# A Trainium2 attention and MoE kernel: the second MoE layer by seven half products, with scaled inputs and one buffer of streaming rows

One core of one Trainium2 chip. The metric is the device time of one launch in microseconds (us); a kernel's time is the median of its runs. PE is TensorE (PEld its weight loads), DVE VectorE, ACT ScalarE, POOL GpSimd; SP is the engine that only issues DMAs here. Groups of tokens and their attentions are numbered from 0: "the second attention" is that of group 2, "the third" that of group 3, and "the second chunk" is group 1. "Turned" means transposed.

## The reference, cut to what matters

```python
# attention: B=4, H=8, S=768, D=64; heads 0, 2, 6 see all earlier rows ("retrieval"),
# the other five see 4 sink rows and a window of 64 rows ("streaming")
x = attention(q, k, v).transpose(0, 2, 1, 3).reshape(3072, 512)
# MoE: E=4 experts, w1[e] 512 x 1024, w2[e] 1024 x 512
p = probs / (probs.sum(-1, keepdims=True) + 1e-9)
for e in range(4):
    h = np.maximum(x @ w1[e], 0.0)
    out += p[:, e:e+1] * (h @ w2[e])
```

## The kernel before

The tokens go in eight groups of 384 (half of a batch entry), three tiles of 128 each. While PE computes the MoE of group g, single steps of the attention of group g+1 are put between its matmuls, paced by a plan. The MoE part:

```python
for g, e in units:                              # 8 groups x 4 experts
    for ft in range(8):                         # first layer: 4 matmuls of 384 columns each
        ... matmul(out=ps[:, 0:384], lhsT=w1sb[...], rhs=xT[g][:, ct, :]) x4
        nc.scalar.activation(out=hs[:, ft, :], in_=ps[:, 0:CH], func=AF.Relu)
    for j in range(3):                          # second layer, tile by tile
        ... matmul(out=ps_o, lhsT=hs[:, ft, tile j], rhs=w2sb[:, e*FTP+ft, :]) x8   # 512 columns
        acc[nt] = p[nt, e] * ps_o (+ acc[nt])   # DVE, one for each tile and expert
```

The attention's data come by cast-loads (they change the type on the way) from POOL's queue and are turned by DMA transposes from SP's queue. The parts (cut):

```python
def dma_transposes(b, c):                # SP: sinks of kSr, q -> qT, kRr -> kR, kSr -> kS
def loads(g2):                           # POOL: k, q, v of group g2
for g in range(G):
    att_steps = attention(g + 1)
    loads(g + 2)
    begin = {0: 1.15, 1: 1.0}.get(g, 0.0) * UNIT     # UNIT: one group and expert, 10.4 us of PE
    end = {0: 3.5}.get(g, 0.90 * n_units) * UNIT
    for ns, share in moe_steps(units[g]):
        ...                              # run attention steps while done < planned share
```

Streaming keys and values have two buffers, q two.

The softmax here doesn't subtract the row's maximum and nothing guards it: scores larger than these inputs give would overflow.

Of the kernel before, what the change touches and what calls it, by code (L numbers as in the profile page):

```python
# [17 lines left out]
def kernel(  # L18
# [34 lines left out]
    P = 128  # L53
# [50 lines left out]
    NR, NSH = len(RH), len(SH)  # L104
    kR = []
    kSf = []
    vR = []
    vSf = []
    for i in range(2):
        kR.append(pers.tile([P, NCH, NR, 3, P], FP16, name=f"kR{i}"))  # L110
        kSf.append(pers.tile([P, NCH * TC * NSH * P], FP16, name=f"kS{i}"))
        vR.append(pers.tile([P, S // P, NR, D + 2], FP16, name=f"vR{i}"))
        vSf.append(pers.tile([P, NT * NSH * P], FP16, name=f"vS{i}"))

    kS = kSf[0].rearrange("p (c s t x) -> p c t s x", c=NCH, t=TC, s=NSH)
    vS = vSf[0].rearrange("p (c s t x) -> p c t s x", c=NCH, t=TC, s=NSH)

    def windows(x, c):

        return x[1 - c][:, 0 : WT * NSH * P].rearrange(  # L120
            "p (t s x) -> p t s x", t=WT, s=NSH
        )

    ident32 = pers.tile([P, P], FP32, name="ident32")
    ident16 = pers.tile([P, P], FP16, name="ident16")
    warm = pers.tile([P, 512], FP16, name="warm")
    bC = pers.tile([P, 2 * P], FP16, name="bC")
    bS = pers.tile([P, 3, TQ], FP16, name="bS")
# [4 lines left out]
    mW = pers.tile([P, WT + 2, WQ], FP16, name="mW")  # L133
# [8 lines left out]
    k_sinks = pers.tile([NS, 1, NSH * P], FP16, name="k_sinks")  # L142
    v_sinks = pers.tile([NS, 1, NSH * P], FP16, name="v_sinks")
# [16 lines left out]
    def key_tile(b, c, h, t):  # L160

        i = b % 2
        if RETR[h]:
            return kR[i][:, t // 3, RH.index(h), t % 3, :]
        if b:
            return windows(kSf, c)[:, t, SH.index(h), :]
        return kS[:, t // TC, t % TC, SH.index(h), :]

    def v_tiles(b, c, h):

        if RETR[h]:
            return vR[b % 2][:, 3 * c : 3 * c + 3, RH.index(h), :]
        if b:
            return windows(vSf, c)[:, :, SH.index(h), :]
        return vS[:, c, :, SH.index(h), :]
# [30 lines left out]
    def load_q(b, c):  # L206
        q16[b, c] = att.tile([P, 3, H, D], FP16, name="q16", bufs=2)
        load_by_rows(q, q16[b, c], b, c)
# [10 lines left out]
    def load_k(b, c):  # L219

        for h in range(H):
# [26 lines left out]
    def dma_transposes(b, c):  # L248
        i = b % 2
        put_sinks(kSr, k_sinks, c)  # L250
        alloc_qT(b, c)
# [6 lines left out]
        for x, xr in ((kR[i][:, c, :, :, :], kRr), (windows(kSf, c), kSr)):  # L258
            nc.sync.dma_start(
                out=x.rearrange("p t s x -> p (t s) x"),  # L260
                in_=xr.rearrange("p t s x -> p (t s x)"),
                transpose=True,
            )
# [24 lines left out]
    def sink_rows(b, c):  # L288
        if b:
            put_sinks(windows(vSf, c), v_sinks, c)  # L290
            return
# [43 lines left out]
    def one_values(eng, c):  # L335

        one_values_r(eng, 0, c)
        x = vS[:, c, :, :, :].rearrange("p t s x -> p s t x")
        fill(eng, x[0:R0, :, :, :].rearrange("p s t x -> p (s t x)"), ONES)
        fill(eng, x[:, 0:2, :, D:P], ONES)  # L340
        fill(eng, x[:, 2:5, :, 0:D], ONES)
# [5 lines left out]
    q32 = moe.tile([P, 3, H, D], FP32, name="q32", tag="hs", bufs=2)  # L347
    k32 = moe.tile([P, 3, H, D], FP32, name="k32", tag="hs", bufs=2)

    v_s32 = pers.tile([NS, H, D], FP32, name="v_s32")  # L350
# [29 lines left out]
    zero(nc.vector, kS[:, 0, :, :, :].rearrange("p t s x -> p s t x"))  # L380
# [42 lines left out]
    def mask_w():  # L423

        gp.memset(mW, 1.0)
# [27 lines left out]
    zero(gp, kS[:, 1, :, :, :].rearrange("p t s x -> p s t x"))  # L453
    one_values(gp, 1)
    k16 = att.tile([P, H, 3, D], FP16, name="k16", bufs=1)
    qt16 = att.tile([P, H, 3, D], FP16, name="q16", bufs=2)
# [38 lines left out]
    def attention(b, c):  # L495
# [3 lines left out]
        xT[g] = att.tile([P, HP, CH], FP16, name="xT", bufs=2)  # L499
# [105 lines left out]
        def scores(h):  # L605
            hp = h // 2
            es_of[h] = []
            for cols, parts, masks in score_tiles(h):
# [22 lines left out]
                es = att.tile([P, 512], FP16, name="es", bufs=12)  # L631
# [77 lines left out]
        def values(h):  # L709
# [31 lines left out]
            if not pair or u == 0:  # L741
                rc_of[0] = att.tile([P, CH], FP32, name="rc", bufs=4)
# [61 lines left out]
        else:  # L804
            sink_rows(b, c)
            order = (0, 2, 6, 1, 3, 5, 7, 4) if by_dma else (0, 2, 1, 3, 6, 5, 7, 4)
            if not by_dma:
# [4 lines left out]
            for n, h in enumerate(order):  # L812
                v_steps = iter(())
                if len(waiting) > (0 if by_dma else 1):
                    v_steps = values(waiting.pop(0))
                yield from both(scores(h), v_steps)
                waiting.append(h)
                if not by_dma and n in (1, 3):
                    yield from transposes({1: 3, 3: 2}[n])
            for h in waiting:  # L820
                yield from values(h)

# [21 lines left out]

    behind = []
# [11 lines left out]
    def last_tile(e, nt, hs, acc):  # L857

        for n, eng in enumerate((nc.sync, nc.scalar)):
            cols = slice(n * DM // 2, (n + 1) * DM // 2)  # L860
            ps = pV.tile([P, 512], FP32, name="pV", bufs=2)
            for ft in range(FTP):
                nc.tensor.matmul(
                    out=ps[:, 0 : DM // 2],
                    lhsT=hs[:, ft, 2 * P : 3 * P],
                    rhs=w2sb[:, e * FTP + ft, cols],
# [3 lines left out]
            nc.vector.scalar_tensor_tensor(  # L870
                out=acc[:, cols], in0=ps[:, 0 : DM // 2],
                scalar=p_sb[:, nt, e : e + 1], in1=acc[:, cols],
                op0=ALU.mult, op1=ALU.add,
            )
            eng.dma_start(out=out[nt * P : (nt + 1) * P, cols], in_=acc[:, cols])


    acc = {}

    def moe_steps(units):  # L880
        for g, e in units:
            nt0 = g * 3
            hs = moe.tile([P, FTP, CH], FP16, name="hs", tag="hs", bufs=2)


            ahead = 4 if g == 0 and e == 0 else 1
            for f0 in [0, *range(ahead, FTP)]:
                pss = {ft: bank() for ft in range(f0, f0 + (1 if f0 else ahead))}


                cts = (0, 2, 1, 3) if g == 0 else (2, 1, 3, 0)

                def layer1(ft, n):
                    ct = cts[n]
                    nc.tensor.matmul(  # L895
                        out=pss[ft][:, 0:CH],
                        lhsT=w1sb[:, e * DMP + ct, ft * P : (ft + 1) * P],
                        rhs=xT[g][:, ct, :],
                        start=(n == 0),
                        stop=(n == DMP - 1),  # L900
                    )

                for ft in pss:
                    for ct in range(DMP - 1):
                        layer1(ft, ct)
                for ft, ps in pss.items():
                    layer1(ft, DMP - 1)
                    nc.scalar.activation(  # L908
                        out=hs[:, ft, :], in_=ps[:, 0:CH], func=AF.Relu
                    )  # L910
                    yield DMP * mm_ns(CH), 0.6
            for j in range(3):
                nt = nt0 + j
                if g == G - 1 and e == E - 1 and j == 2:
                    last_tile(e, nt, hs, acc[nt])
                    continue
                ps_o = pO.tile([P, DM], FP32, name="pO", bufs=2)
                for ft in range(FTP):
                    nc.tensor.matmul(  # L919
                        out=ps_o,  # L920
                        lhsT=hs[:, ft, j * P : (j + 1) * P],
                        rhs=w2sb[:, e * FTP + ft, :],
                        start=(ft == 0),
                        stop=(ft == FTP - 1),
                    )
                    if ft == FTP // 2 - 1:
                        yield FTP // 2 * mm_ns(DM), 1.4
                p_ap = p_sb[:, nt, e : e + 1]
                if e == 0:
                    acc[nt] = moe.tile([P, DM], FP32, name="acc", bufs=6)  # L930
                    nc.vector.tensor_scalar(  # L931
                        out=acc[nt], in0=ps_o, scalar1=p_ap, scalar2=None, op0=ALU.mult
                    )
                else:
                    nc.vector.scalar_tensor_tensor(  # L935
                        out=acc[nt], in0=ps_o, scalar=p_ap, in1=acc[nt],
                        op0=ALU.mult, op1=ALU.add,
                    )
                if e == E - 1:
                    nc.sync.dma_start(out=out[nt * P : (nt + 1) * P, :], in_=acc[nt])  # L940
                yield FTP // 2 * mm_ns(DM), 1.4
# [10 lines left out]
    mask_w()  # L952

    units = {g: [(g, e) for e in range(E)] for g in range(G)}

    def loads(g2):
# [79 lines left out]
```

## Time and profile before

| | before |
|---|---|
| median time | 399.19 us (398.47 to 400.19, 3 runs) |
| span of the profiled run | 397.1 us, clock 1.000 |
| PE, PEld, DVE, ACT, POOL busy | 98%, 56%, 39%, 55%, 36% |

The busy shares, the stretches and the bare pace of the matmuls are shown and read in the prediction below. One more number is used throughout, and is worked out from the trace: for each matmul the time to the start of the next one, less columns/2.4 + 2.5 ns. I call the sum of columns/2.4 + 2.5 **issue**, and the rest **lost**. Before: 385.1 us of issue, 12.0 us lost, 4.9 of it in the first 22 us and 3.6 after the last matmul. One thing in these figures is not as that rule says: the 24 fp32 transposes of the first 22 us were counted with four times their columns, though they go by in some 109 ns each (median), twice what 128 columns take. Counted plainly, 3.8 us move from issue to lost (before: 381.3 and 15.7 us).

### The profile page before, as it was taken

The numbers are of one execution on the slowest core, as the hardware profiler recorded it, in microseconds if no ns is written. First come the engines' busy times: TensorE is split into PE (matmuls) and PEld (weight loads), VectorE is DVE, ScalarE is ACT, GpSimd is POOL, SyncE is SP. The second block draws the span as 40 slices with busy tenths as digits, with TensorE's granted clock in tenths as the row PEclk, the third lists the DMA queues.
The fourth block names the chain that finished last, engine by engine and source line by source line (L and its number), as shares of the span: only waits on it lengthen the run. The fifth ranks groups of instructions, "written<-read, shape, count | busy, mean of one in ns | idle before, by whom it ended". The sixth has DMA issues, their size and how long they took to land.

```text
span 397.1 us, 7140 instructions
## 1 busy us (share of the span) xinstructions
PE 388.2 (98%) x2829; PEld 220.7 (56%) x2829; DVE 156.0 (39%) x344; ACT 219.0 (55%) x468; POOL 143.7 (36%) x184
## 2 busy tenths in 40 slices
PE   7899999999999999999999999999999999999996
PEld 4654556545555555555555555555555555555553
DVE  7734765324442234434332333433443223422222
ACT  4754569444766546655765446745564456853331
POOL 8833796808908706900049202940000000000000
PEclk9999999999999999999999999999999999999999
DMA  9999999999999999970779959990472000020002
GB/s 172 158 208 192 178 197 172 139 199 128 128 191 149 121 149 106 141 90 12 141 80 175 65 99 118 112 153 12 83 117 83 2 12 1 11 79 2 0 2 80
DMA packets 166133, 42.23 MB, mean 106 GB/s; under 512 B 156396, under 2 KB 161108, under 8 KB 166100
## 3 DMA queue, kind: packets, MB, share of 16 engines
q0 software_dynamic: 102656, 20.98, 62.0%
q1 hardware_dynamic: 61700, 20.27, 26.5%
q10 hardware_dynamic: 1744, 0.52, 0.6%
q8 instruction: 22, 0.36, 0.4%
q14 instruction: 11, 0.09, 0.1%
HBM read 43.57 MB, written 6.29 MB: 126 GB/s over the span
## 4 chain that ended last, share of the span: by engine, by line
PE 78%; DMA 15%; POOL 6%; issue 1%; DVE 0%; POOLq 0%
PE pA L895 35%; PE pO L919 35%; DMA w1sb<-in_moe_w_dram 4%; DMA w2sb<-in_moe_w_dram 4%; PE pA L614 4%; DMA q<-in_q_dram 3%; DMA kR<-kRr 2%; POOL vR L269 2%; PE pV L726 1%; PE pV L662 1%; DMA vS<-in_v_dram 1%; POOL w1sb L300 1%; POOL vS L275 1%; POOL vS L326 0%; POOL q L201 0%
## 5 line engine op out<-in xcount | busy, mean ns | idle before, releaser
L895 PE MATMUL pA<-xT,w1sb 128*128 128x384 f16 x1024 | 185.9, 326 | 0.1
L919 PE MATMUL pO<-w2sb,hs 128*128 128x512 f16 x760 | 179.0, 379 | 0.8 <-DMA w2sb<-in_moe_w_dram 0.8
L908 ACT ACTIVATE hs<-pA 128x384 f16<-128x384 f32 x256 | 121.8, 492 | 94.9 <-PE pA L895 89.6
L895 PEld LDWEIGHTS <-w1sb 128*128 128x128 f16 x1024 | 95.8, 98 | 59.6 <-issue 0.5
L919 PEld LDWEIGHTS <-hs 128*128 128x128 f16 x760 | 70.7, 98 | 73.9 <-DMA w2sb<-in_moe_w_dram 1.2
L632 ACT ACTIVATE es<-pA 128x384 f16<-128x384 f32 (+2 forms) x122 | 60.1, 512 | 53.7 <-PE pA L614 52.4
L935 DVE SCALAR_TENSOR_TENSOR acc<-pO,p_sb,acc 128x512 f32<-128x512 f32 x71 | 53.3, 751 | 71.8 <-PE pO L919 71.3
L227 POOL DMA_DIRECT2D kSr<-in_k_dram x30 | 30.1, 1006 | 31.5 <-DMA kS<-kSr 22.1
L223 POOL DMA_DIRECT2D kRr<-in_k_dram x18 | 14.1, 785 | 67.7 <-DMA kR<-kRr 67.7
L749 DVE TENSOR_TENSOR xT<-pV,rc 64x384 f16<-64x384 f32 x37 | 20.5, 554 | 32.0 <-ACT rc L754 24.3
L271 POOL DMA_DIRECT2D vS<-in_v_dram x30 | 30.4, 1024 | 0.8 <-DMA q<-in_q_dram 0.8
L931 DVE TENSOR_SCALAR acc<-pO,p_sb 128x512 f32<-128x512 f32 x24 | 18.0, 751 | 28.8 <-PE pO L919 28.6
L636 DVE TENSOR_TENSOR es<-es,mC 128x256 f16<-128x256 f16 (+1 forms) x42 | 10.9, 258 | 45.4 <-ACT es L632 44.3
L744 ACT ACTIVATE rc<-pV,eps 64x384 f32<-64x384 f32 x37 | 21.3, 575 | 12.1 <-PE pV L726 11.5
L614 PE MATMUL pA<-qT,kR 128*128 128x384 f16 (+2 forms) x120 | 24.4, 278 | 0.9 <-ACT qT L525 0.4
L754 ACT ACTIVATE rc<-rc 64x384 f32<-64x384 f32 x38 | 19.8, 521 | 1.2
L269 POOL DMA_DIRECT2D vR<-in_v_dram x24 | 19.2, 802 | 0.4 <-issue 0.3
L726 PEld LDWEIGHTS <-vS 128*128 128x128 f16 x255 | 13.4, 98 | 7.7 <-DMA vS<-in_v_dram 2.1
L636 DVE TENSOR_TENSOR es<-es,mW 128x384 f16<-128x384 f16 x30 | 10.7, 358 | 16.9 <-ACT es L632 16.8
L614 PEld LDWEIGHTS <-kR 128*128 128x128 f16 x120 | 11.4, 98 | 10.6 <-DMA kR<-kRr 0.6
L662 PEld LDWEIGHTS <-es 128*128 128x128 f16 x252 | 13.2, 97 | 6.9 <-ACT es L632 0.6
L614 PEld LDWEIGHTS <-kS 128*128 128x128 f16 x255 | 13.3, 98 | 6.6
(102 smaller groups left out, 188.4 us busy)
## 6 DMA issues: line engine op xcount, KB each, us to landing
out_dram<-acc SPq DMA_DIRECT2D x23, 256.0 KB
w1sb<-in_moe_w_dram POOLq DMA_DIRECT2D x8, 512.0 KB, 9.4
w2sb<-in_moe_w_dram POOLq DMA_DIRECT2D x4, 1024.0 KB, 13.2
kSr<-in_k_dram POOLq DMA_DIRECT2D x30, 112.0 KB, 3.8
vS<-in_v_dram POOLq DMA_DIRECT2D x30, 112.0 KB, 5.6
q<-in_q_dram POOLq DMA_DIRECT2D x18, 128.0 KB, 4.3
vR<-in_v_dram POOLq DMA_DIRECT2D x24, 48.0 KB, 4.4
kRr<-in_k_dram POOLq DMA_DIRECT2D x18, 48.0 KB, 3.7
```

The costliest lines, as they stand in the source:

```text
L227: gp.dma_start(out=kSr[:, :, SH.index(h), own(h)], in_=windows_of(k, b, h, c),)
L269: gp.dma_start(out=t[:, :, 0:D], in_=rows_of(v, b, h, c))
L271: gp.dma_start(out=t[:, :, own_v(h)], in_=windows_of(v, b, h, c))
L614: nc.tensor.matmul(out=ps[:, o : o + nq], lhsT=key_tile(b, c, h, t), rhs=qTs[b, c][:, hp, q0 : q0 + nq], start=(n == 0 or not first), stop ...
L632: nc.scalar.activation(out=es[:, 0:cols], in_=ps[:, 0:cols], func=AF.Exp, scale=SC)
L636: nc.vector.tensor_tensor(out=es[:, o0:o1], in0=es[:, o0:o1], in1=m[:, mo : mo + o1 - o0], op=ALU.mult,)
L744: nc.scalar.activation(out=rc[r, :], in_=ps[o, 0:CH], func=AF.Ln, bias=eps[o, :])
L749: nc.vector.tensor_tensor(out=xT[g][r, ct, :], in0=ps[r, 0:CH], in1=rc[r, :], op=ALU.mult)
L895: nc.tensor.matmul(out=pss[ft][:, 0:CH], lhsT=w1sb[:, e * DMP + ct, ft * P : (ft + 1) * P], rhs=xT[g][:, ct, :], start=(n == 0), stop=(n = ...
L908: nc.scalar.activation(out=hs[:, ft, :], in_=ps[:, 0:CH], func=AF.Relu)
L919: nc.tensor.matmul(out=ps_o, lhsT=hs[:, ft, j * P : (j + 1) * P], rhs=w2sb[:, e * FTP + ft, :], start=(ft == 0), stop=(ft == FTP - 1),)
L935: nc.vector.scalar_tensor_tensor(out=acc[nt], in0=ps_o, scalar=p_ap, in1=acc[nt], op0=ALU.mult, op1=ALU.add,)
```

## The change

Twenty of the 24 tiles are done in ten pairs. The inputs of a pair are multiplied by the expert's probability before the first layer (this may be done ahead of the Relu, as probabilities are not negative), so all four experts can be summed in one accumulation, and the second layer becomes one product of a 256 x 4096 by a 4096 x 512 matrix. That one is done as 2 x 2 blocks by seven half products in place of eight (Strassen's method in Winograd's form). The new matrices need memory: streaming keys and values and q get one buffer each in place of two, score buffers go from 12 to 8, those of the reciprocals (`rc`) from 4 to 2, and the sums of the first four tiles share memory with the blocks.

```diff
-    for i in range(2):
-        kSf.append(pers.tile([P, NCH * TC * NSH * P], FP16, name=f"kS{i}"))
-        vSf.append(pers.tile([P, NT * NSH * P], FP16, name=f"vS{i}"))
+    kSf = pers.tile([P, NT * NSH * P], FP16, name="kS")
+    vSf = pers.tile([P, NT * NSH * P], FP16, name="vS")
+    tsb = pers.tile([P, 3, KT, HN], FP16, name="tsb")        # sums of weights
+    hA = pers.tile([P, 6 * KT * P], FP16, name="hA")         # A11 A21 A12 A22 S1 S2
-        q16[b, c] = att.tile([P, 3, H, D], FP16, name="q16", bufs=2)
+        q16[b, c] = att.tile([P, 3, H, D], FP16, name="q16", bufs=1)
-                es = att.tile([P, 512], FP16, name="es", bufs=12)
+                es = att.tile([P, 512], FP16, name="es", bufs=8)
... attention: values follow one head behind; keys of the next group are turned inside it
+                if n == 3 and more and g > 1:
+                    transpose_rows(*more)                    # q, retrieval keys
+            if more:
+                if g == 1:
+                    transpose_rows(*more)
+                transpose_windows(*more)                     # streaming keys, at its end
... the pairs
+        for e in range(E):
+            if e + 1 < E:
+                scale_inputs(nt0, e + 1)                     # DVE: xs = xT * p
+            if e == E - 1 and nxt is not None:
+                load_probs(nxt)                              # SP
+            for f0 in range(0, FTP, 2):  # 8 matmuls of 256 columns, one Relu of 512
+            if e == 1:
+                input_sums(0, 2 * HT)                        # DVE: S1, S3, S2
+            elif e > 1:
+                input_sums(e * HT, (e + 1) * HT)
+        yield from product(x, A11, b(0, 0), True);   keep(0, x)
+        yield from product(y, A12, b(1, 0), True);   ... S4 = A12 - S2; add(0, y, 0, 0)
+        yield from product(x, S2, t(1), False);      keep(1, x); scale_inputs(nxt, 0)
+        yield from product(y, S1, t(0), True);       keep(2, y)
+        yield from product(x, S3, b(0, 1), False);   add(2, x, 1, 1)
+        yield from product(y, S4, b(1, 1), False);   add(1, y, 0, 1)
+        yield from product(x, A22, t(2), False);     copy, store
... order of the MoE: first group plainly, one tile plainly, ten pairs
+        load_probs(pairs[0])
+        for e in range(E):
+            yield from plain_steps(3, 1, e, lambda: xT[1][:, :, 0:P], n0)
+            last_weight_sum(e)
+            if e == E - 1:
+                scale_inputs(pairs[0], 0)
... the plan of the attentions
+    begin = E * UNIT
+    for a, n in zip(range(2, G), (0.6, 1.65, 3.2, 4.65, 6.2, 7.65)):
+        plan[a] = (begin, first_pair + n * PAIR)
+        begin = plan[a][1]
```

## The prediction

> **What bounds the kernel now.** I read the page's busy shares first, then the table of stretches, then the chain of waits in order of time, then the groups by shape. The busy shares:
>
> ```profile
> PE 388.2 (98%) x2829; PEld 220.7 (56%) x2829; DVE 156.0 (39%) x344; ACT 219.0 (55%) x468; POOL 143.7 (36%) x184
> ...
> PE 78%; DMA 15%; POOL 6%; issue 1%; DVE 0%; POOLq 0%
> ```
>
> PE is busy for 98% of the span, no other engine for more than 56%. The second line is the chain that ended last: 78% of it is PE. A busy PE is not yet a PE at its peak, because a pipelined matmul looks long, so I look for stretches where the pace can be counted. The stretches (length, then busy time and count of PE, weight loads, DVE, ACT, POOL, then the clock):
>
> ```profile
> core 0: us, PE busy (x) PEld busy (x) DVE busy (x) ACT busy (x) POOL busy (x), PEclk, DMA share, GB/s
> 0.00:10.00 10.00, 7.80 (x56) 4.56 (x56) 7.75 (x21) 4.32 (x10) 8.78 (x21) 1.00 1.01 171
> 40.00:60.00 20.00, 20.00 (x179) 11.57 (x178) 14.17 (x31) 12.29 (x28) 16.94 (x27) 1.00 1.25 190
> 220.00:260.00 40.00, 40.00 (x316) 22.72 (x315) 15.87 (x35) 22.08 (x46) 15.60 (x18) 1.00 1.02 101
> 352.00:394.00 42.00, 41.47 (x232) 22.45 (x230) 9.95 (x14) 15.68 (x32) 0.00 (x0) 1.00 0.06 24
> ```
>
> From 40 us on PE has no gap, at clock 1.00. The last group of 384 tokens has no attention beside it, so the chain shows the pace bare (start, length, what):
>
> ```profile
> 351.93 5.20 PE pA L895 x32
> 357.13 5.18 PE pO L919 x24
> ...
> 391.73 1.76 PE pV L863 x16
> ```
>
> 5.20/32 = 162.5 ns for 384 columns, 5.18/24 = 215.8 ns for 512, 1.76/16 = 110 ns for 256: each is columns/2.4 + 2.5 ns. So PE issues at its full rate, and the number of columns streamed is the cost. Check: L895 1,024 x 162.5 = 166.4 us, L919 760 x 215.8 = 164.0, L863 16 x 110 = 1.8; the two MoE layers are 332.2 us. The attention's matmuls, counted by their shapes the same way, are some 53 us. With about 6 us before PE runs and 3.6 us from the last matmul (393.5) to the end (397.1) that makes 395 of 397 us. There is almost no stall to win; only fewer streamed columns help.
>
> **What the Trainium skill says.** "TensorE: Matmul & The Clock Gate", section "Wait — 56ns, not 53.3ns?", gives a warm start-to-start of N/2.4 + about 2.5 ns; the three numbers above agree. The same page under "Back-to-back issue gap" says a stream of load-and-matmul pairs sustains about 131 ns at N=512; this trace has 215.8 ns, and I use the trace. "VectorE: DVE Perf Modes", "The perf-mode tier table", says that a two-input operation runs at two elements a cycle when all is 16-bit in SBUF and at one with fp32 or PSUM. The trace agrees:
>
> ```profile
> L749 DVE TENSOR_TENSOR xT<-pV,rc 64x384 f16<-64x384 f32 x37 | 20.5, 554 | 32.0 <-ACT rc L754 24.3 <-PE pA L614 3.8 <-PE pV L726 1.9
> L636 DVE TENSOR_TENSOR es<-es,mW 128x384 f16<-128x384 f16 x30 | 10.7, 358 | 16.9 <-ACT es L632 16.8
> L632 ACT ACTIVATE es<-pA 128x512 f16<-128x512 f32 x48 | 28.0, 598 | 30.5 <-PE pA L614 30.2 <-PE pA L626 0.2
> L632 ACT ACTIVATE es<-pA 128x256 f16<-128x256 f32 x22 | 8.4, 383 | 7.9 <-PE pA L614 7.6 <-PE pA L626 0.3
> L870 DVE SCALAR_TENSOR_TENSOR acc<-pV,p_sb,acc 128x256 f32<-128x256 f32 x2 | 1.0, 484 | 0.5 <-PE pV L863 0.4
> ```
>
> Columns: engine, operation, shapes, count, then busy us and mean ns of one, then idle before it. 384 elements take 358 ns all in f16, 554 ns with an f32 input. Taking 0.52 and 1.04 ns an element for the two modes (half of 1/0.96 and 1/0.96) leaves about 158 ns fixed for both. ACT from PSUM: (598-383)/256 = 0.84 ns an element, and about 168 fixed.
>
> **The change on PE.** Four tiles of 128 tokens keep the old way, 20 tiles go in ten pairs.
> - Group of three tiles: first layer 128 x 162.5 = 20.8 us, second 96 x 215.8 = 20.7.
> - The single tile: first layer 128 matmuls of 128 columns at 55.8 (the formula) = 7.1, second 32 x 215.8 = 6.9.
> - A pair: first layer 128 matmuls of 256 columns x 109.2 = 14.0 us; second layer 7 products x 16 matmuls of 256 columns = 112 x 109.2 = 12.2 us, in place of 64 x 215.8 = 13.8. Ten pairs: 262.0.
>
> Sum 317.6 us against 332.2: **14.6 us less**. Note that the eighth saved in the second layer of a pair (13.65 to 11.95 us of bare streaming) is mostly kept: matmuls of 256 columns pay the 2.5 ns twice as often, and that is small. Weight loads are no hindrance: in the trace runs of seven 54-column matmuls pass in about 0.2 us, each with its own load. The attention streams what it did (53 us); one transpose of the probabilities adds 0.3.
>
> **The change on DVE and ACT, per pair.** Scaling the inputs: four of 1,024 elements with an f32 factor, 4 x 1.22 = 4.9 us. Sums S1, S3, S2: three of 1,024 elements and six of 512 in f16, 3 x 0.69 + 6 x 0.42 = 4.6. S4: 2 x 0.69 = 1.4. Three final adds at the 484 ns of the row above: 1.5. Together 12.4 us. It loses 8 evictions of 751 ns (two tiles, four experts) = 6.0. A pair with its share of attention is about 30 us of PE, and attention needs about 6 us of DVE in it, so DVE rises from 39% to about 60%: still not the bound. ACT: 16 Relus x 598 + 3 x 383 = 10.7 us against two thirds of 32 x 492 = 10.5. Equal. Over the first layer alone it has 9.6 us plus some 5 of attention beside 16 us of PE; the old first layer was as full (598/874 against 492/650).
>
> **What lands on the path.**
> - From the single tile to the first pair: behind the last matmul DVE must evict (0.75), take the last weight difference in place (0.69, it waits for those matmuls) and scale the first inputs (1.22), all emitted after the tile ends. PE waits about **2.7 us**, once.
> - In the single tile a Relu of 128 columns takes 168 + 128 x 0.84 = 275 ns against four matmuls in 223, with attention's exponentials beside it: about **1 us** over the tile.
> - Inside a pair: product 4 overwrites a PSUM buffer that DVE reads after one S4 half: 0.2 + 0.69 + 0.48 + 0.15 = 1.5 us, while product 3 runs 1.75 us. It just fits; with the odd attention operation in between I allow 0.1 us a pair, **1 us**.
> - Attention between 97 and 240 us is denser and DVE comes in bursts of up to 3.3 us (two sums and a scaling), so a mask can hold a value product: **1 us**.
>
> Sum: 399.2 - 14.6 + 2.7 + 1 + 1 + 1 = 390.3, so **390.3 us**.
>
> **Rivals.**
> 1. **Single buffers become a wait.** Keys of the streaming heads can be transposed only after the previous attention's last scores, and SP is held 5.4 to 8.4 us by that transpose in the trace. For: PE issues in order, and a late key stops it. Against: retrieval heads come first, and three of eight heads spread over 27 us or more give over 8 us; the probabilities for the next pair are requested some 14 us before PE must have them. If it bites at six attentions, 1 us each: 396.
> 2. **DVE becomes the bound in the pairs.** For: 12.4 us of new work in an engine that runs in order. Against: 60% busy, and every sum has a product or more of slack. If its waits cost 0.7 us more a pair: 397, which is "same".
> 3. **All is hidden**, the 2.7 us too, as attention matmuls are put in that gap: 399.2 - 14.6 = 384.6, the floor.
> 4. **Loading in the first 85 us.** DMA engines are above 90% there, and a queue of loads that waits for a single q buffer could start the second attention late. The first weight loads are unchanged and the keys now go ahead of the sinks, so I expect no change; +3 us at worst.
>
> **Range and chances.** The saving is counted, not guessed, so the doubt lies in the waits: 0 to 11 us. Range 385.0 to 396.0. The border of 2% is 391.2, only 0.9 above my number. Since the order of work looks arranged so that each wait falls behind a product, I put faster at 0.58, same at 0.39, slower at 0.03.
>
> **What the changed profile would show.** Right: matmuls of 256 columns in bare stretches at 109 ns, the last pair at 26.2 us, PE without gaps but one of some 2.7 us where the first scaled inputs are awaited; DVE near 220 us busy. Wrong: repeated PE idle before the products with DVE as releaser (rival 2), before scores with a key transpose (rival 1), a pace of 256-column matmuls above 112 ns (weight loads bind), or a granted clock under 1.00.

## More of the kernel before

`begin` for g = 1 says that the attention of group 2 starts one UNIT after the MoE of group 1 has begun. In the attention of group 1, the only one turned by PE transposes after the first, the values of a head follow its scores at a distance of two heads; 12 score buffers (`es`) allow that.

## The result

The changed kernel takes **409.8 us** (409.45 to 410.45, 4 runs) against 399.38 us for the kernel before (now 4 runs): 2.7% slower. A ratio here is the mean time of one kernel's runs over that of the other's in the same rounds, so not quite the ratio of the medians: 1.027, 95% interval 1.025 to 1.029. Executions over 1.5% slower than the fastest of the same kernel are left out of the means. The predicted range ended at 396.0.

The busy shares and the chain that ended last, from the page of the changed kernel:

```profile
PE 380.9 (93%) x3814; PEld 314.4 (77%) x3814; DVE 220.5 (54%) x472; ACT 231.1 (57%) x476; POOL 138.9 (34%) x182
...
PE 48%; DVE 6%; ACT 5%; issue 1%; ACTq 0%
```

PE has fewer busy microseconds than before (380.9 against 388.2) in a longer span, and DVE and ACT have come into the chain. So the work did shrink, and PE waits. Where, the stretches show (length, busy time and count of PE, PEld, DVE, ACT and POOL, then the granted clock as a share of the full one, and what the DMA engines did):

```profile
80.00:90.00 10.00, 3.62 (x31) 3.37 (x32) 1.36 (x3) 2.15 (x7) 5.72 (x11) 0.67 1.21 117
...
100.00:125.00 25.00, 21.50 (x244) 17.77 (x243) 15.20 (x28) 16.13 (x37) 10.98 (x15) 0.93 1.76 128
125.00:250.00 125.00, 122.74 (x1344) 108.62 (x1342) 68.20 (x150) 80.47 (x156) 50.48 (x57) 1.00 1.23 128
...
350.00:378.00 28.00, 27.55 (x253) 24.47 (x251) 12.52 (x22) 11.21 (x21) 0.00 (x0) 1.00 0.14 48
```

Between 80 and 90 us PE works 3.6 us of 10, and the clock falls to 0.67. The rest is nearly full. The timeline of PE names the two large waits (start, length, instruction, count, and in brackets the idle time before and what ended it):

```profile
86.38 0.61 PE L627 MATMUL pA<-qT,kR 128*128 128x128 f16 x2 [7.89 <-DMA kR<-kRr]
86.78 3.19 PE L947 MATMUL pA<-xT,w1sb 128*128 128x128 f16 x28
...
106.94 1.61 PE L1049 MATMUL pA<-xs,w1sb 128*128 128x256 f16 x8 [2.58 <-DVE xs L1025]
```

The first scores of the second attention wait 7.89 us for its retrieval keys; the 28 matmuls behind run at about 107 ns each and not at 55.8, half the pace. The matching line of PE's timeline of the kernel before:

```profile
85.67 0.39 PE L614 MATMUL pA<-qT,kR 128*128 128x128 f16 x2 [0.17 <-DMA kR<-kRr]
```

There the keys came 0.7 us earlier (85.67 against 86.38), and PE asked for them just then. Issue and lost time by stage:

| stage | before: lost | after: lost | what the largest waits are, after |
|---|---|---|---|
| start to 22 us | 4.9 | 5.0 | |
| to the end of the first three tiles (74.3; 78.1) | 1.5 | 4.9 | exponentials and masks of the second chunk's attention |
| single tile, to the first pair (106.9) | – | 13.1 | keys 8.05, first scaled inputs 2.74, slow clock 2.0 |
| all that follows, to the last matmul | 2.0 | 10.9 | scaled inputs in the pairs 5.2, attention 3.7, slow clock |
| after the last matmul | 3.6 | 3.1 | |
| **lost, all** | **12.0** | **37.0** | |
| **issue, all** | **385.1** | **370.7** | |
| span | 397.1 | 407.7 | |

14.4 us of issue are saved, against the 14.6 less 0.3 that the prediction counted; 25.0 us more are lost. The prediction had 5.7 us for new waits; the other 19 us are its whole error.

### The profile page after: what moved, and what is told of

The parts are those of the page before. It is cut to its first block, busy times and chain, and to the rows that moved or that the text cites. A ratio compares the mean times of both kernels' runs of the same rounds, so it can differ in the third digit from the quotient of the medians.

```text
span 407.7 us, 9337 instructions
## 1 busy us (share of the span) xinstructions
PE 380.9 (93%) x3814; PEld 314.4 (77%) x3814; DVE 220.5 (54%) x472; ACT 231.1 (57%) x476; POOL 138.9 (34%) x182
## 4 chain that ended last, share of the span: by engine, by line
PE 48%; DVE 6%; ACT 5%; issue 1%; ACTq 0%
PE pO L1078 25%; PE pA L1049 19%; ACT hA L1058 3%; DVE hA L916 3%; PE pA L627 2%; DVE xs L1025 2%; DVE hA L1031 1%; ACT es L645 1%; PE pV L675 1%; PE pV L739 1%; ACT rc L757 1%; DVE es L649 0%; ACT rc L767 0%; ACT o L1137 0%; ACTq L1137 0%
## 5 line engine op out<-in xcount | busy, mean ns | idle before, releaser
L1049 PE MATMUL pA<-xs,w1sb 128*128 128x256 f16 x1280 | 154.9, 274 | 6.7 <-DVE xs L1025 6.7
L1049 PEld LDWEIGHTS <-w1sb 128*128 128x128 f16 x1280 | 121.6, 98 | 23.6 <-DVE xs L1025 9.2
L1058 ACT ACTIVATE hA<-pA 128x512 f16<-128x512 f32 x160 | 94.6, 598 | 42.5 <-PE pA L1049 38.3
L1078 PEld LDWEIGHTS <-hA 128*128 128x128 f16 x1120 | 107.1, 98 | 12.8
L1078 PE MATMUL pO<-w2sb,hA 128*128 128x256 f16 x640 | 76.3, 272 | 0.0
L1078 PE MATMUL pO<-tsb,hA 128*128 128x256 f16 x480 | 58.2, 273 | 0.0
L1025 DVE TENSOR_TENSOR xs<-xT,pB 128x1024 f16<-128x1024 f16 (+1 forms) x52 | 49.4, 972 | 8.3 <-PE pA L1049 8.2
L916 DVE TENSOR_TENSOR hA<-hA 128x1024 f16<-128x1024 f16 (+1 forms) x80 | 41.8, 553 | 3.8 <-PE pO L1078 2.6
L947 PE MATMUL pA<-xT,w1sb 128*128 128x384 f16 (+1 forms) x256 | 33.6, 283 | 0.1
L968 PE MATMUL pO<-w2sb,hA 128*128 128x512 f16 x128 | 31.3, 381 | 0.6 <-DMA w2sb<-in_moe_w_dram 0.6
L947 PEld LDWEIGHTS <-w1sb 128*128 128x128 f16 x256 | 21.1, 103 | 8.6 <-issue 0.7
L762 DVE TENSOR_TENSOR xT<-pV,rc 64x384 f16<-64x384 f32 x37 | 20.5, 554 | 11.4 <-ACT rc L767 9.1
```

Source lines behind the costliest of these rows:

```text
L916: nc.vector.tensor_tensor(out=out, in0=a, in1=b, op=ALU.subtract)
L947: nc.tensor.matmul(out=pss[ft][:, 0:cols_n], lhsT=w1sb[:, e * DMP + ct, ft * P : (ft + 1) * P], rhs=x[:, ct, :], start=(n == 0), stop=(n = ...
L968: nc.tensor.matmul(out=ps_o, lhsT=hs[:, ft, j * P : (j + 1) * P], rhs=w2sb[:, e * FTP + ft, :], start=(ft == 0), stop=(ft == FTP - 1),)
L1025: nc.vector.tensor_tensor(out=o, in0=xin, in1=pb.to_broadcast([P, DMP, n, P]), op=ALU.mult)
L1049: nc.tensor.matmul(out=ps[:, f * PC : (f + 1) * PC], lhsT=w1sb[:, e * DMP + ct, (f0 + f) * P : (f0 + f + 1) * P], rhs=xs[:, ct, :], start= ...
L1058: nc.scalar.activation(out=blocks[:, b0 : b0 + 2, k0 : k0 + 2, :].rearrange("p t f x -> p f t x"), in_=ps.rearrange("p (f t x) -> p f t x" ...
```

## The experiments

Theory A: the saving is real, and is lost to an order of work that asks for data too early. Mostly this is one number of the plan: the second attention starts at `E * UNIT`, with the single tile, while the kernel before starts it one UNIT later. Rival B: the loads and transposes are simply too slow for a shorter kernel, and a mended wait will come back elsewhere. Rival C: DVE is too full.

### The start alone, in the kernel before

```diff
-        begin = {0: 1.15, 1: 1.0}.get(g, 0.0) * UNIT
+        begin = {0: 1.15}.get(g, 0.0) * UNIT
```

> The kernel before, with one number altered: the second attention begins one unit (10.4 us) earlier, at the start of the second group, as the changed kernel has it. Nothing of the seven products is in it. Theory A: PE asks for keys at about 74.5 us that land at 85.6 us: a wait of 10 to 11 us with the key transpose as releaser, the clock falls behind it (1 to 3 us): 408 to 412 us. Rival: the wait in the changed kernel comes from its single buffers and load order, so here the keys come sooner or other work fills in: under 403 us.

Measured: 409.95 us, ratio 1.027. From the stretches and PE's timeline of this run:

```profile
80.00:90.00 10.00, 5.00 (x18) 2.55 (x19) 0.29 (x1) 2.10 (x5) 0.99 (x2) 0.51 1.51 237
...
85.00 0.61 PE L614 MATMUL pA<-qT,kR 128*128 128x128 f16 x2 [9.88 <-DMA kR<-kRr]
85.40 4.05 PE L895 MATMUL pA<-xT,w1sb 128*128 128x384 f16 x12
```

With none of the seven products in it, the kernel before becomes as slow as the changed one, by the same wait: PE stands 9.88 us for the same keys, and the clock halves. Double buffers do not prevent it. That a start too early costs about 10 us is shown; that it is all of the changed kernel's loss is not, since that kernel has its own waits beside it.

### A later start, and the order of loading, in the changed kernel

```diff
 # e1_late
-    begin = E * UNIT
+    begin = E * UNIT + 0.65 * ONE          # ONE: the single tile, 14.05 us of PE
 # e2_qfirst
-        load_k(b, c, SH)
-        load_q(b, c)
+        load_q(b, c)
+        load_k(b, c, SH)
```

> The changed kernel (409.8 us), with one number altered: the second attention begins 0.65 of the single tile later (about 9 us of matmuls). Theory A (too early a start): the first scores then come at about 87 us, just behind the key transpose that lands at 86.4 us. The 8.05 us wait of PE goes to under 1 us, the 2 to 3 us of slowed clock behind it go too: 399 to 400 us. Rival B (loading): the loads as a whole are late, and the wait only moves to streaming keys, v or the next attention: 405 to 410 us, with a DMA as releaser of a later PE wait.

Measured: 405.85 us, ratio 1.016. The wait for keys is gone, but only 4 us are won. The time lies inside rival B's range, and as B says, a wait has moved with a transfer at its root; but the transfer is not the streaming rows that B names. DVE's and SP's timelines of this run:

```profile
103.16 2.36 DVE L1025 TENSOR_TENSOR xs<-xT,pB 128x1024 f16<-128x1024 f16 x2 [7.53 <-DMA pB<-p_rows]
...
89.80 5.74 SPq L255 DMA_TRANSPOSE kS<-kSr  x1
95.64 2.23 SPq L989 DMA_DIRECT2D out_dram<-hA  x3
97.92 0.42 SPq L1009 DMA_DIRECT2D pB<-p_rows  x1
```

The scaling of the first pair's inputs waits for probabilities (`pB`) whose load SP issued only at 97.92 us, behind a transpose that kept SP for 5.74 us and stores behind that. In the changed kernel, where SP issued this load at 95.45 us, this second wait lay under the first.

> The changed kernel, with the q rows loaded ahead of the streaming keys. Theory A says the first scores wait for what is landed last of q and retrieval keys, and SP sat 8.7 us waiting for q (landed 76.2 us): with q some 5 us earlier the transposes start about 4 us earlier, the 8.05 us wait becomes 3 to 5 us: 405 to 406.5 us. Rival B (the load engines are simply full, order does not matter): the wait stays above 7 us: 409 to 410.5 us.

Measured: 408.31 us, ratio 1.022; between the two expectations. q landed at 75.4 us in place of 77.9, but the keys, whose transpose was issued at 77.7, came only at 85.2; the value loads that POOL issued from 74.2 us on were landing until 88.5. PE's wait was 6.64 us in place of 8.05. That the order did this is not shown: with the old order it was 6.66 us in the profiled run of `e3_sums_later`, whose edit acts later. What is left for the order are the 1.5 us of the median. Whatever the kernel, where PE asked early the first scores ran at 85 to 88.3 us: 86.4 in the changed kernel, 85.2 here, 85.8 in `e3_sums_later`, 88.3 in `e4_first_xs`, 85.0 in `b1_early2`.

### Probabilities ahead of the transposes

```diff
 # f1_probs, on top of e1_late
             if e == 1:
                 turn_probs()
+            if e == 3:
+                load_probs(pairs[0])
...
-        load_probs(pairs[0])
```

> The run with the later second attention (405.85 us, where the wait for keys was gone but PE waited 10.4 us for the first scaled inputs, and DVE 7.5 us of it for the probabilities that SP issued only at 97.9 us behind a key transpose), with the load of those probabilities issued one expert earlier in the first group, ahead of the transposes. Theory A' (two waits in a row on the same SP queue and the same early start): both are gone, the scaled-input wait is back at 2.7 us; 405.85 - 7.6 - about 1.5 of slowed clock = 396.5 to 398.5 us. Rival B (loads are late as such): another DMA wait of 4 us or more appears between 80 and 125 us: 402 us or more.

Measured: 403.63 us, ratio 1.009. The expectation is missed, and the total lies in the rival's range, but the four runs spread: 399.74 for the profiled one, 403.3 to 404.63 for the others. In the profiled run the stretch from the single tile to the first pair loses 3.0 us in place of 13.1, of which 2.77 is the predicted wait for the first scaled inputs. What the three slower runs waited for has no trace and stays open. I suspect the loads, since the runs below show new waits for them in that region.

### Order on DVE, inside the pairs and before the first

The last pair but one of the changed kernel, with no attention beside it, from its chain in order of time (start, length, what):

```profile
357.94 0.61 ACT hA L1058
358.57 0.70 DVE hA L1031
359.30 1.29 DVE hA L916 x2
360.60 1.22 DVE xs L1025 x2
361.86 3.67 PE pA L1049 x32
365.52 12.23 PE pO L1078 x112
```

The last Relu of expert 1, the sums S1, S3 and S2 of experts 0 and 1, then the scaling for expert 3, one behind the other: 3.9 us, while the first layer of expert 2 gives cover for 3.5. PE loses 0.62 us by it here, and 0.57 to 1.08 us in seven of the ten pairs. The seven products themselves take 12.23 us for 112 matmuls, 109.2 ns each, with no wait.

```diff
 # e3_sums_later
             if e + 1 < E:
                 scale_inputs(nt0, e + 1)
+            if e == 2:
+                input_sums(0, 2 * HT)
...
-            if e == 1:
-                input_sums(0, 2 * HT)
-            elif e > 1:
+            if e > 1:
 # e4_first_xs
+            if e == E - 1:
+                scale_inputs(pairs[0], 0)
             yield from plain_steps(3, 1, e, ...)
             last_weight_sum(e)
-            if e == E - 1:
-                scale_inputs(pairs[0], 0)
```

> The changed kernel; only the order on DVE is altered: the sums of experts 0 and 1 are issued behind the scaling of the inputs for expert 3, not ahead of it. Theory A: PE's waits for scaled inputs inside pairs (0.57 to 1.08 us each, about 5.2 us in ten pairs) end: 404.5 to 405.5 us. Rival C (DVE is too full): the same backlog comes out before the third product or at the attention's masks, and the total stays: 408.5 to 410 us.

Measured: 404.3 us, ratio 1.011, 0.2 us under theory A's range (in the profiled run the wait for keys was 1.4 us shorter too). The waits for scaled inputs inside the pairs are gone, and the last pair runs bare (chain of this run; two lines of code were added above, so L1049 is L1051):

```profile
371.69 13.97 PE pA L1051 x128
385.66 12.24 PE pO L1078 x112
```

13.97 + 12.24 = 26.2 us, the predicted pair to a tenth. Rival C falls: the order was wrong, not the load too high.

> The changed kernel; the first pair's inputs for expert 0 are scaled before the last expert of the single tile and not after it. My prediction put a wait of 2.7 us there and the trace has 2.74: Theory A says it goes, 407 us (and a little of the slowed clock). Rival: the probabilities in row form are not there yet (SP issued that load at 95.4 us), DVE stalls in order and attention's masks with it: no change, 409 to 410.5 us.

Measured: 405.1 us, ratio 1.014. In the profiled run the wait of 2.74 us is gone, but that for keys was 9.42 us there (407.23 us); the other runs were 404.04 to 405.89. The mechanism is confirmed, the size not: 407 us was expected, and the median fell by 4.7 us, more than the wait that went; the three faster runs have no trace.

### All repairs together, and q first

> Later second attention, early probabilities, sums behind the scaling, first scaling one expert earlier: all repairs. By the table of lost issue time: 370.7 us of issue + 5.0 start + 4.9 first group + 1 single tile + 5 pairs + 3.1 tail = 389.7 us of span, 391.7 us of time, 2% under the kernel before. If the repairs overlap in what they win (rival), 394 to 397 us.

Measured: 400.85 us, ratio 1.005: short of the hoped 391.7, and above the rival's range too. From the single tile to the first pair only 0.8 us are lost now, and the third attention now asks too early. PE's and SP's timelines of this run:

```profile
123.07 0.61 PE L627 MATMUL pA<-qT,kR 128*128 128x128 f16 x2 [5.23 <-DMA kR<-kRr]
...
111.86 3.91 SPq L268 DMA_TRANSPOSE qT<-q  x3
115.81 2.31 SPq L255 DMA_TRANSPOSE kR<-kRr  x1
```

The key transpose stands behind that of q; q's load stood behind the streaming keys on POOL; and those had to wait for their one staging buffer (the kernel before has one, too) until the transpose before had landed, at 100.9 us. So q first (`g1_all_q` is `f2_all` with the edit of `e2_qfirst`):

> As f2_all (400.85 us), with the q rows loaded ahead of the streaming keys in every group. In f2_all the third attention asked for its retrieval keys at 117.7 us and they landed at 123.1: their transpose stood behind that of q, whose load stood behind the streaming keys, whose staging buffer came free only at 100.9 us. Theory A'' (a chain of loads made too short by the denser start): that wait of 5.4 us and its slowed clock (1.9 us) go: 393 to 394.5 us, 1.3% under the kernel before. Rival B (the load engines are full): the wait moves to streaming keys or v, 398 us or more.

Measured: 397.36 us (393.34 to 398.95, 6 runs), ratio 0.994, interval 0.991 to 0.998: between the two expectations, a miss by 3 us in the median, with one run as hoped. The spread is wider than that of the kernel before (398.1 to 400.7); what the slower runs waited for has no trace and stays open. The 5.4 us wait is gone. What is left there is 2.55 us for streaming keys at 100.8 us.

### What the seven products are worth by themselves

In the mended schedule, the second layer of a pair by 64 matmuls of 512 columns; scaled inputs and experts summed in PSUM stay, the sums on DVE go:

```diff
-        yield from product(x, A11, b(0, 0), True)        # ... seven of them
+        for i in range(PT):
+            ps = pO.tile([P, DM], FP32, name="pO", bufs=2)
+            for m in range(E * FTP):
+                ... matmul(out=ps, lhsT=blk, rhs=w2sb[:, m, :])
+            nc.scalar.copy(out=o[:, i, :], in_=ps)
```

> As f2_all, but the pairs' second layer by 64 matmuls of 512 columns in place of seven half products of 16 matmuls of 256: inputs still scaled, experts still summed in PSUM, no sums of inputs or weights. My working: 64 x 215.8 = 13.81 us against 112 x 109.2 = 12.23 us a pair, so 15.8 us more than f2_all over ten pairs, less what the sums cost in waits there. If the seven products pay as counted: 13 to 16 us more than f2_all. Rival: their DVE sums and PSUM hand-overs eat most of it: under 8 us more.

Measured: 412.23 us, 11.4 us over `f2_all`, less than expected: `f2_all` carried the third attention's wait, and lost 15.5 us in the stretch of the pairs against 8.2 here. With q first in both:

> As g1_all_q without the seven half products (64 matmuls of 512 columns a pair). With the loading waits out of both, the counted 15.8 us should show as 14 to 16 us more than g1_all_q: 407 to 410 us. If less than 10 us, the products cost more on other engines than I think.

Measured: 413.42 us (412.48 to 414.45, 4 runs), 16.1 us over `g1_all_q`. The difference is at the upper edge of the expectation; the absolute time missed it, since `g1_all_q` itself was slower than hoped. The issue time of the two differs by 15.9 us (386.6 against 370.7), as counted. In a mended order the seven products keep their whole gain. It also shows that scaling inputs and summing experts in PSUM, without the seven products, win nothing here: the issue time is 1.5 us above that of the kernel before, and the kernel is 3.6% slower, though it still gives up the memory and has a wait of 3.5 us for streaming keys in it.

### Values one head behind

In the kernel before, nothing else changed:

```diff
-                if len(waiting) > (0 if by_dma else 1):
+                if waiting:
```

> The kernel before, with the second chunk's attention (the only one by PE transposes) taking up the values of a head one head after its scores and not two, as the changed kernel must with 8 score buffers for 12. The changed kernel lost 4.9 us in the first group against 1.5. If the shorter distance is the cause: 1 to 3 us more than the kernel before (400.5 to 402.5 us), with PE waits for exponentials and masks between 45 and 75 us. Rival (the weight sums on DVE hold the masks): no change, 399 to 399.8 us.

Measured: 402.41 us, ratio 1.009, 3.6 us more, a little above what I expected. PE's timeline of this run has, among others,

```profile
64.70 0.27 PE L726 MATMUL pV<-es,vS 128*128 128x160 f16 x2 [0.35 <-DVE es L636]
...
72.74 0.27 PE L726 MATMUL pV<-es,vS 128*128 128x160 f16 x2 [0.63 <-DVE es L636]
```

waits of the length that the changed kernel has (0.35 and 0.63 us there too), where the kernel before has none: 4.1 us lost in the first group (1.5 before, 4.9 changed). So the distance is worth 2.6 of the 3.4 us there; of the rest, 0.7 us is a wait for streaming keys at 51 us that neither the kernel before nor this run has. Four buffers fewer for scores are what forces it. In the changed kernel (`h2_lag2`) the four buffers were given back for this attention only, from the slot of the output tiles, unused until the pairs; and in `h1_later` the second attention was begun later still:

```diff
 # h2_lag2, on top of g1_all_q
+                if g == 1 and n_es[0] % 3 == 2:
+                    es = es_more[:, n_es[0] // 3 % 4, :]      # slot of "o"
...
-                if waiting:
+                if len(waiting) > (0 if by_dma else 1):
 # h1_later, on top of g1_all_q
-    begin = E * UNIT + 0.65 * ONE
+    begin = E * UNIT + 0.9 * ONE
-    ... (0.6, 1.65, 3.2, ...)
+    ... (0.7, 1.65, 3.2, ...)
```

> g1_all_q with four more score buffers for the second chunk only (in the slot of the output tiles, unused until the pairs) and the values two heads behind, as in the kernel before. If the buffers are the cause: the first group's lost time falls from 5.1 to 1.5 to 2.5 us, total 393.5 to 395 us. But an earlier end of that group asks for the keys earlier, so 1 to 3 us may come back as key waits (then 395 to 397.5 us). If the weight sums on DVE are the cause: first group unchanged, 397 us.

Measured: 395.07 us, ratio 0.988. The first group's loss falls from 5.1 to 2.4 us; the wait for streaming keys grew from 2.55 to 4.6, as PE now comes earlier.

> g1_all_q (397.36 us) with the second attention begun another quarter of the single tile later (3.5 us) and stretched to 0.7 of the first pair. Theory A (start too early for the loads): the wait of 2.55 us for streaming keys at 100.8 us, 1.1 us behind it and the slowed clock of 100 to 110 us go: 393 to 394.5 us. Rival B (load engines full): the wait comes at a later key or v, 396.5 us or more.

Measured: 400.18 us (398.89 to 404.12), ratio 1.003: a miss, in the rival's range. The wait for streaming keys is gone, and one of the same kind has replaced it. ACT's and SP's timelines:

```profile
102.17 1.09 ACT L1060 ACTIVATE hA<-pA 128x512 f16<-128x512 f32 x2 [6.52 <-DMA out_dram<-hA]
...
88.32 6.41 SPq L255 DMA_TRANSPOSE kS<-kSr  x1
94.83 2.34 SPq L989 DMA_DIRECT2D out_dram<-hA  x4
```

The Relu of the first pair writes where the sums of the plainly computed tiles still lie, and their stores, three of them ready by 79.5 us and the fourth by 93.7, were issued by SP only after the transpose. This is the price of the shared memory.

> Both: 390 to 392 us, about 2% under the kernel before (398.9 us), near the 390.3 us that I predicted for the change as it was. If the loads bind from there on: 394 to 396 us.

Measured: 395.84 us (394.22 to 400.99), ratio 0.990: short of 390 to 392 and in the range said for loads that bind, with that same wait (4.7 us at 99.3 us).

### The stores from another queue

```diff
 # i1_act_store, on top of h3_both, in the plainly computed tiles
-                nc.sync.dma_start(out=out[...], in_=acc[nt])
+                nc.scalar.dma_start(out=out[...], in_=acc[nt])
```

> h3_both (395.84 us) with the four stores of the plainly computed tiles issued from ACT's queue. If the order on SP is the cause: the wait of 4.7 us at 99 us and its slowed clock (1 to 2 us) go: 389 to 391.5 us, 2 to 2.5% under the kernel before. If the load engines are the cause, the stores land as late from the other queue or the keys are late in their place: 394.5 us or more.

Measured: **392.26 us** (391.13 to 397.97, 6 runs), ratio 0.985, interval 0.981 to 0.988: 1.5% under the kernel before, and 4% under the changed one. The median is 0.8 us above the expected range. The page and the stretches of this run:

```profile
PE 376.1 (97%) x3814; PEld 312.7 (80%) x3814; DVE 219.5 (56%) x472; ACT 230.4 (59%) x476; POOL 138.0 (35%) x182
...
80.00:90.00 10.00, 10.00 (x119) 7.47 (x118) 5.08 (x7) 5.52 (x24) 6.84 (x12) 1.00 1.71 187
90.00:100.00 10.00, 10.00 (x103) 8.46 (x101) 6.35 (x17) 6.83 (x15) 1.31 (x2) 1.00 1.38 125
```

PE is full where it stood still, at clock 1.00, so rival B, that the load engines are too slow, does not hold there. Lost time is 18.7 us of a span of 389.4. The new queue has a price: the three early stores wait in it ahead of a Relu, and PE loses 1.5 us at 77.8 us. And 395.47 and 397.97 us among the six runs say that some wait still comes and goes; they have no trace. The gain of 14.4 us in issue is thus kept but for 6.7, and all outputs of all kernels here were correct.

## Why the prediction was wrong, point by point

- **The saving on PE: right.** Predicted 14.6 less 0.3 us, measured 14.4; 256 columns at 109.2 ns, a bare pair at 26.2 us; weight loads no hindrance.
- **Costs on DVE: right.** 1,024 elements in f16 took 0.69 us and 512 took 0.42, as predicted, and a scaling of 1,024 with the f32 factor 1.22; DVE was busy for 220.5 us. The 0.52 ns an element can be had from the two rows shown there: (554 - 358)/384 = 0.51.
- **"From the single tile to the first pair ... 2.7 us, once": right**, 2.74 us. But I did not see that the probabilities stand behind the transposes on SP; in `e1_late` this made the wait 10.4 us.
- **Rival 4, "I expect no change; +3 us at worst": this is the step that failed.** I asked only whether the loads would come later, and took it that the second attention starts at the same moment in both kernels. The loads did come nearly as before; the start is what moved. The profile before has its first scores at 85.7 us, after a wait of 0.17 us for these same keys, and the code before says `1: 1.0`; the new plan says `E * UNIT`, one UNIT less. I had both and did not lay one beside the other. It cost 8.05 us and about 2 of slow clock at once. `b1_early2` shows that number alone at 10.7 us.
- **Rival 1, single buffers, "1 us each": right in kind, wrong in size and place.** In the trace the loads of the second attention's retrieval keys and q wait for no buffer. The third's do, for the staging buffer (`f2_all`, 5.4 us); so do the blocks in `h1_later`, for the memory that they share with sums not yet stored (PE 5.7 us).
- **"Every sum has a product or more of slack": wrong.** I named a DVE burst of 3.3 us (by my own terms three sums and a scaling, not two), but only as a thing that holds a mask, and left out the Relu that it waits for, 0.6 us. The sum was 3.9 against a cover of 3.5, and 5.2 us went in the ten pairs.
- **Score buffers: missed.** The prediction does not name the step from 12 to 8 and what it does to the distance of scores and values: 2.6 us of the 3.4 that the first group lost more (`b2_lag1`).
- **"Inside a pair: 1 us" for the hand-over of PSUM: too much.** No product waited. "Attention ... 1 us" was 3.7; no experiment says why, and the two `rc` buffers that went were not tested. The single tile's ACT bound of 1 us was about 0.2 where the clock was full. The "some 53 us" of attention have 5.9 us of warm-up matmuls in them and the fp32 transposes four times; plainly counted the attention is 43 us. As it stands on both sides, it does no harm.
- **Slow clock: missed.** I had listed a clock under 1.00 as a sign of error, and it is one here, but I gave it no term. The Trainium skill, "TensorE: Matmul & The Clock Gate", "Part 1: The HAM clock gate", says that PE falls to half rate when idle for a window and needs sustained work to come back; the 107 ns behind the wait agree.

## What to carry to other kernels

A saving counted in matmuls is only as good as the plan that starts the other work; when an order of work is replaced, lay each start of old and new side by side on the old trace, and see what was just in time. A saturated PE hides waits under each other: each one mended shows the next, often in the same in-order DMA queue. And where memory was the price, look at what shares it, since a buffer given up comes back as a wait somewhere that the diff does not name.

## What the Trainium skill lacked or had wrong

- "TensorE: Matmul & The Clock Gate", "Back-to-back issue gap": about 131 ns sustained for load-and-matmul pairs at N=512. Measured here: 215.8 ns at 512 columns, 109.2 at 256, as its isolated formula has it.
- The same page, "Part 1: The HAM clock gate": idle of a window of about 3.4 us brings the slow clock. Here an idle time of 2.60 us before the first pair (`f1_probs`) was already followed by a clock of 0.50 from 97 to 100 us.
- "DMA: Bandwidth & Descriptors", "DMA Transpose (X-bar)": nothing on how long the issuing queue is held. One transpose of 35 blocks of 128 x 128 held SP's queue 5.2 to 8.8 us in these traces, one of nine blocks 1.3 to 4.0, and everything behind waited. (Elsewhere the page has sequencer cycles of transposes, in a part on another chip and its forerunners.)
- No page that I found has the delay of an SP transpose under load: keys of nine blocks, issued at 77.7 us, were there at 85.2 while POOL's cast-loads were landing (`e2_qfirst`).
